# Retention into a mixture of experts on one core: the decay multiplication of both tiles of a pair put behind both tiles' outputs, one-hots and weight splits put behind the masks, and k of the first four tiles turned on TensorE

## The chip, the cores and the metric

The kernel runs on one core of a Trainium2 chip. The metric is device time in microseconds (us), from the start of the program on the core to its end; a smaller one is better. In the tables of the profile the engines are PE (TensorE, the matmuls), PEld (TensorE's weight loads), DVE (VectorE), ACT (ScalarE), POOL (GpSimd) and SP (the engine that issues the DMAs of this kernel).

## What is computed

The output of a retention layer (causal attention without softmax, with a decay gamma^(i-j) for each head) goes as tokens into a mixture of eight experts, one expert for each token.

```python
def _attn_ref(q, k, v):                      # batch 8, heads 8, seq 576, head_dim 64
    scores = scale * np.matmul(q, k.transpose(0, 1, 3, 2))
    gamma = 1.0 - 2.0 ** (-5.0 - np.arange(H))
    rel = pos[:, None] - pos[None, :]
    Dmat = np.where(rel >= 0, gamma[:, None, None] ** rel[None, :, :], 0.0)
    return np.matmul(scores * Dmat[None, :, :, :], v)

def _moe_ref(x, expert_emb, tau, w1, w2):    # x: 4608 tokens of 512
    logits = xn @ en.T / tau
    expert_idx = np.argmax(logits, axis=1)
    gate_w = probs[np.arange(N), expert_idx]
    for e in range(E):                       # 8 experts, w1 512x1024, w2 1024x512
        mask = expert_idx == e
        h = np.maximum(x[mask] @ w1[e], 0.0)
        out[mask] = gate_w[mask, None] * (h @ w2[e])
    return out
```

## The kernel before

The 4608 tokens are 36 tiles of 128 rows, nine tiles to two batches of 576 (tile 4 of the nine lies half in each batch). The retention takes the tiles in 18 **pairs**: pair s holds the tiles t = 2s and u = 2s + 1. All operands are float32. q and k come transposed (`qkt`, 512 KB for a tile), k and v also as rows (`kvt`, 512 KB for a tile: k in half 0, v in half 1). The steps for a tile, by the functions' names:

- `emit_A` (scores): TensorE multiplies k and q into two banks of PSUM, pa[0] and pa[1] for an even tile, pa[2] and pa[3] for an odd one; then VectorE multiplies each bank by the triangle `tri` (L614, the **masks**, four for a pair) into SBUF.
- `emit_U` (state): TensorE adds k-rows times v to the running state in the bank `pst`; ScalarE copies it to `T` (L690). v has been scaled by gamma^-i before, by GpSimd (`scale_v`, L597).
- `emit_QT` and `emit_O` (output): TensorE adds T times q, and the masked scores times v, in `po`. `po` is one tile of two banks, and each bank holds halves of both tiles of the pair.
- `emit_X` (L700): VectorE multiplies the output in `po` by the decay `gsb` into `xT` in SBUF. This is **the decay multiplication**.
- `emit_T`: TensorE turns `xT` back to rows (L134, into `prow` and pa[3]), ScalarE copies them (L716) and squares them (L719), and a DMA stores them in `xd` (L717).

In pair s the program writes: loads of the tiles t+5 and u+5, `scale_v` of t+2 and u+2, A of t+2 and u+2, QT of t and u, U of u, O of t, X of t, O of u, U of t+2, X of u, then T of the pair before. Loads, `scale_v` and A thus run ahead of the outputs. The order within an engine is the order of this text (`manual_schedule`); the waits between engines are set by the framework from the tiles that an instruction reads and writes.

Between these steps stand **jobs**, hung at a place (pair, slot) by `at` and run by `do`: slot 0 is ahead of the loads, slot 1 behind A, slot 2 behind the outputs, slot 3 at the end of the pair. They route the tokens, group by group of four or five tiles: logits (TensorE), turn and head (VectorE), rank, `route_onehot` (VectorE, L315, L323, L330: the **one-hots**) and `route_table` (TensorE). Four more are **weight splits**: ScalarE rounds a quarter of the first expert's w1 (L191), VectorE forms the rest (L192). Three prepare the experts' embeddings (square, a sum on TensorE, scale). In front of the loop stand tile 0 and A of tile 1; A of the tiles 2 and 3 is in pair 0.

Behind the retention come the experts: gather tokens, two layers of matmuls for each expert, scatter. The change doesn't touch them.

Of the kernel before, what the change touches and what calls it, by code (L numbers as in the profile page):

```python
# [47 lines left out]
LAST = 2  # L48
KT = 9
NLOAD = 7  # L50
PORD = (0, 2, 1, 3)


# [40 lines left out]
def retention_moe(ctx: ExitStack, tc: tile.TileContext, qk, kv, embT, tau, w1, w2, cst, out):  # L94
# [389 lines left out]
    with ExitStack() as att:  # L484
# [12 lines left out]
        def load_qk(t):  # L497
            qkt[t] = qkp.tile([P, NP, 2, P], F32, name="qkt")
            nc.sync.dma_start(out=qkt[t], in_=qk[t])

        def load_kv(t):
            kvt[t] = qkp.tile([P, 2, H, D], F32, name="kvt")
            nc.sync.dma_start(out=kvt[t], in_=kv[t])

        emb = ap.tile([P, NP, NE], F32, name="emb")
        taub = ap.tile([P, 1], F32, name="taub")
# [4 lines left out]
        nc.sync.dma_start(out=cs[:, _FIRST:], in_=cst[:, _FIRST:])  # L511
        load_kv(1)
        load_qk(2)
        nc.sync.dma_start(out=emb, in_=embT)
        nc.sync.dma_start(out=taub, in_=tau.rearrange("(o n) -> o n", o=1).broadcast_to([P, 1]))
        load_kv(2)
        for t in range(3, NLOAD):
            load_qk(t)
            load_kv(t)

# [16 lines left out]
        nc.vector.memset(E32, 0.0)  # L537
        nc.gpsimd.memset(vx[:D], 0.0)
        nc.vector.tensor_scalar(out=tri, in0=iota, scalar1=part, scalar2=None, op0=ALU.is_ge)

        def constants():
            nc.vector.tensor_scalar(out=ident, in0=iota, scalar1=part, scalar2=None, op0=ALU.is_equal)
            nc.vector.tensor_copy(trix, tri)
            nc.vector.memset(trix[:D, D:], 0.0)
            nc.vector.tensor_scalar(out=stri, in0=iota, scalar1=part, scalar2=None, op0=ALU.is_gt)
            nc.vector.tensor_scalar(
                out=wme, in0=iota[:, :NE], scalar1=-1.0, scalar2=float(NE), op0=ALU.mult, op1=ALU.add
            )
            nc.vector.tensor_scalar(out=entry[:, :, 0], in0=iota[:, :NT], scalar1=1.0, scalar2=None, op0=ALU.add)
            nc.vector.tensor_scalar(  # L550
                out=entry[:, :, 1], in0=iota[:, :NT], scalar1=0.0, scalar2=part, op0=ALU.mult, op1=ALU.add
            )
# [68 lines left out]
        def out_rows(p, h):  # L621

            o = h ^ (p & 1)
            return slice(o * D, (o + 1) * D)

        opened = set()

# [135 lines left out]
                f()  # L763

        at((0, 3), constants)
        at((0, 3), lambda: (embeddings_square(), embeddings_sum()))
        at((1, 3), embeddings_scale)
        for b in range(B - 1):
            t0, G = group_tiles(b)
            s0 = (t0 + G - 1) // 2 + 1  # L770
            if b < B - 2:
                at((s0, 2), lambda b=b: route_logits(b))
                at((s0, 3), lambda b=b: (route_turn(b), route_head(b)))
                at((s0 + 1, 3), lambda b=b: (route_rank(b), route_onehot(b)))
                at((s0 + 2, 3), lambda b=b: route_table(b))
            else:
                at((s0 - 1, 3), lambda b=b: route_logits(b))
                at((s0, 1), lambda b=b: (route_turn(b), route_head(b)))
                at((s0, 3), lambda b=b: (route_rank(b), route_onehot(b)))
                at((s0 + 1, 1), lambda b=b: route_table(b))  # L780
                at((s0 + 1, 1), lambda: slots_to_tokens(0, 3))
                for i in range(3):
                    at((s0 + 1, 1), lambda i=i: gather(0, i, group_tiles(B - 1)[0] * P))
                at((s0 + 1, 1), route_bump)
        for i, (load, split) in enumerate(wsplit_steps(0, wrp)):
            at((5 + 2 * i, 0), load)
            at((8 + 2 * i, 3), split)

        def loads(t):
            if t < NT:  # L790
# [1 line left out]
                load_kv(t)  # L792

        emit_A(0)
        scale_v(0, nc.vector)
        emit_U(0)
        decay(0)
        scale_v(1, nc.gpsimd)
        decay(1)
        emit_A(1)  # L800
        for s in range(NT // 2):
            t, u = 2 * s, 2 * s + 1
            do(s, 0)
            if s > 0:
                loads(t + NLOAD - 2)
                loads(u + NLOAD - 2)
                scale_v(t + 2, nc.gpsimd)
                scale_v(u + 2, nc.gpsimd)
                for k in (t + 2, u + 2):
                    if k < KT:  # L810
                        decay(k)
                if s < NT // 2 - 1:
                    emit_A(t + 2)
                    emit_A(u + 2)
            else:
                scale_v(2, nc.gpsimd)
                scale_v(3, nc.gpsimd)
                decay(2)
                decay(3)
            psm.banks = [prow]  # L820
            do(s, 1)
            psm.banks = [pa[2], pa[1], pa[0]]
            emit_QT(t)
            emit_QT(u)
            emit_U(u)
            emit_O(t)
            emit_X(t)
            emit_O(u)
            emit_U(t + 2)
            emit_X(u)  # L830
            if s == 0:
                emit_A(2)
                emit_A(3)
            do(s, 2)
            if s > 0:
                emit_T(t - 2)
                emit_T(u - 2)
            do(s, 3)
# [352 lines left out]
```

## Time and profile before

| | |
|---|---|
| time, median of 3 runs | 638.23 us (637.53 to 641.52) |
| the profiled execution: time | 638.23 us |
| the profiled execution: span of its instructions | 636.4 us |
| PE busy | 591.1 us (93%) |
| PEld busy | 527.6 us (83%) |
| DVE, ACT, POOL busy | 318.8, 223.0, 191.1 us |
| HBM read, written | 82.08 MB, 19.94 MB |

The span is that of the instructions in the trace; 1.8 us of the execution lie outside it. The retention takes about the first 195 us, the experts the rest. A busy matmul's end is modelled, so weight loads (PEld), which stand ahead of each matmul, tell more exactly where TensorE has nothing to do.

### The profile page before, as it was taken

The page shows a single profiled execution, that of the slowest core. Times are in us where ns is not written, and L with a number is a line of the kernel's source. Part 1 is how long each engine was busy: PE and PEld are TensorE (multiplying, and loading weights), DVE is VectorE, ACT ScalarE, POOL GpSimd, SP SyncE. Part 2 cuts the span into 40 slices and gives each one's busy share as a digit, 9 for nine tenths or more (in the row PEclk, how much of TensorE's full clock was granted, in tenths as well). Part 3 has the DMA queues.
Part 4 walks back from the last instruction along what each step waited for, and adds up shares of the span by engine and source line. Part 5 has one row for each costly group of instructions (what it writes and reads, how often), then busy time and mean ns, then how long its engine had stood idle before and what let it go on. Part 6 is the DMA issues. An engine that isn't in the chain of part 4 may idle for free.

```text
span 636.4 us, 12682 instructions
## 1 busy us (share of the span) xinstructions
PE 591.1 (93%) x5154; PEld 527.6 (83%) x5154; DVE 318.8 (50%) x626; ACT 223.0 (35%) x427; POOL 191.1 (30%) x184
## 2 busy tenths in 40 slices
PE   7798887787778999999999999999999999999995
PEld 6677776676656989998898899899889899989985
DVE  3456565756652757857147417626724633731200
ACT  1043423333524325624242425432623434241211
POOL 3743123112114175540450314234235032320002
PEclk8799997989987999999999999999999999999998
DMA  8768886687415296968429616737725651910001
GB/s 309 303 234 313 322 301 260 231 316 295 154 50 183 76 246 175 301 144 194 149 80 205 217 42 154 247 105 155 249 80 145 171 200 41 195 74 35 2 8 70
DMA packets 76324, 111.89 MB, mean 176 GB/s; under 512 B 44971, under 2 KB 45263, under 8 KB 76241
## 3 DMA queue, kind: packets, MB, share of 16 engines
q1 hardware_dynamic: 68560, 90.74, 45.4%
q0 software_dynamic: 7680, 19.95, 9.8%
q8 instruction: 63, 1.03, 0.6%
q14 instruction: 21, 0.16, 0.1%
HBM read 82.08 MB, written 19.94 MB: 160 GB/s over the span
## 4 chain that ended last, share of the span: by engine, by line
PE 66%; issue 15%; DVE 10%; DMA 3%; ACT 3%; POOL 3%; SPq 1%; POOLq 0%; DVEq 0%; ACTq 0%
PE pa L130 20%; PE o L926 20%; PE po L130 7%; PE prow L130 7%; PE pst L130 6%; PE pa L926 3%; DVE raw L614 3%; DVE xT L700 2%; DVE wslot L192 2%; PE prow L134 2%; PE pa L134 1%; DMA kvt<-kv 1%; POOL out L934 1%; DMA raw<-raw 1%; POOL gt L393 1%
## 5 line engine op out<-in xcount | busy, mean ns | idle before, releaser
L926 PE MATMUL o<-wslot,hs 128*128 128x512 f32 (+1 forms) x816 | 186.6, 384 | 0.5 <-ACT y L933 0.4
L926 PEld LDWEIGHTS o<-wslot,hs 128*128 128x128 f32 x816 | 148.6, 188 | 29.5 <-ACT y L933 0.8
L130 PE MATMUL pa<-xs,wslot 128*128 128x256 f32 (+4 forms) x912 | 132.9, 298 | 0.0
L130 PEld LDWEIGHTS pa<-xs,wslot 128*128 128x128 f32 x912 | 127.3, 190 | 0.9
L934 POOL DMA_INDIRECT out<-y,sid x40 | 43.5, 1088 | 223.3 <-ACT y L933 208.2
L192 DVE TENSOR_TENSOR wslot<-raw,wslot 128x1024 fp32r<-128x1024 f32 x64 | 78.6, 1233 | 32.2 <-ACT wslot L191 31.5
L866 DVE SCALAR_TENSOR_TENSOR hs<-pa,hs 128x384 fp32r<-128x384 f32 (+1 forms) x76 | 35.7, 477 | 104.5 <-ACT hs L865 104.5
L597 POOL TENSOR_TENSOR kvt<-kvt,cs 128x512 f32<-128x512 f32 x35 | 36.9, 1055 | 106.0 <-DMA kvt<-kv 83.0
L191 ACT CAST wslot<-raw 128x1024 fp32r<-128x1024 f32 x64 | 66.4, 1048 | 6.0 <-DMA raw<-w 5.4
L865 ACT ACTIVATE hs<-pa 128x256 fp32r<-128x256 f32 (+1 forms) x76 | 32.3, 433 | 98.6 <-PE pa L130 90.1
L382 POOL DMA_INDIRECT raw<-xd,gid x40 | 43.3, 1082 | 78.3 <-DVE wslot L192 29.6
L130 PE MATMUL po<-raw,kvt 128*64 128x128 f32 (+1 forms) x640 | 42.4, 281 | 22.9 <-DVE xT L700 21.3
L933 ACT ACTIVATE y<-o,gt 128x512 f32<-128x512 f32 (+1 forms) x34 | 22.6, 674 | 106.7 <-PE o L926 93.7
L130 PEld LDWEIGHTS po<-raw,kvt 128*64 128x64 f32 x640 | 34.4, 146 | 27.7 <-DVE xT L700 24.9
L130 PE MATMUL prow<-xs,wslot 128*128 128x320 f32 (+4 forms) x336 | 55.5, 314 | 0.2 <-issue 0.2
L130 PEld LDWEIGHTS prow<-xs,wslot 128*128 128x128 f32 x336 | 51.9, 188 | 1.4 <-issue 0.5
L690 ACT COPY T<-pst 128x256 f32<-128x256 f32 x32 | 11.9, 372 | 108.5 <-PE pst L130 108.5
L393 POOL DMA_INDIRECT gt<-gd,gid x40 | 45.3, 1133 | 12.2 <-issue 12.2
L130 PE MATMUL pa<-qkt 64*128 64x128 f32 x576 | 44.6, 294 | 3.8 <-ACT lt L739 1.1
L130 PEld LDWEIGHTS pa<-qkt 64*128 64x128 f32 x576 | 39.4, 199 | 8.2 <-DVE L_all L749 2.1
L614 DVE TENSOR_TENSOR raw<-pa,tri 128x512 f32<-128x512 f32 x64 | 40.0, 682 | 10.2 <-PE pa L130 10.2
L700 DVE TENSOR_TENSOR xT<-po,gsb 128x512 f32<-128x512 f32 x36 | 24.8, 690 | 39.2 <-PE po L130 37.9
(140 smaller groups left out, 605.3 us busy)
## 6 DMA issues: line engine op xcount, KB each, us to landing
raw<-w SPq DMA_DIRECT2D x64, 512.0 KB, 4.3
qkt<-qk SPq DMA_DIRECT2D x36, 512.0 KB, 5.9
kvt<-kv SPq DMA_DIRECT2D x36, 512.0 KB, 6.6
xd<-y SPq DMA_DIRECT2D x36, 256.0 KB, 2.2
raw<-xd,gid POOLq DMA_INDIRECT x40, 3.6
gt<-gd,gid POOLq DMA_INDIRECT x40, 4.3
out<-y,sid POOLq DMA_INDIRECT x40, 3.1
raw<-raw SPq DMA_TRANSPOSE x37, 3.7
```

The costliest lines, as they stand in the source:

```text
L130: pe[:] = [nc.tensor.matmul(*args, **kw)]
L191: nc.scalar.copy(hi, raw)
L192: nc.vector.tensor_tensor(out=sl[:, 1, c * 1024 : (c + 1) * 1024], in0=raw, in1=hi.bitcast(F32), op=ALU.subtract)
L382: return nc.gpsimd.indirect_dma_start(out=t[:, :DM], out_offset=None, in_=xd[:rows, :], in_offset=bass.IndirectOffsetOnAxis(ap=gid[:, a : ...
L393: nc.gpsimd.indirect_dma_start(out=g[:, i : i + 1], out_offset=None, in_=gd[:, :], in_offset=bass.IndirectOffsetOnAxis(ap=gid[:, a : a + 1 ...
L597: eng.tensor_tensor(out=v, in0=v, in1=gneg[:, t % KT].unsqueeze(2).broadcast_to([P, H, D]), op=ALU.mult)
L614: nc.vector.tensor_tensor(out=pm[:, h], in0=banks[h].rearrange("p (c n) -> p c n", c=NP), in1=m.unsqueeze(1).broadcast_to([P, NP, P]), op= ...
L700: nc.vector.tensor_tensor(out=xg4[b][:, g], in0=po[:, :, t % 2], in1=gsb[:, t % KT].rearrange("p (o r) n -> p o (r n)", o=2), op=ALU.mult,)
L865: a = nc.scalar.activation(hi, ps[:, :n], AF.Relu)
L866: v = nc.vector.scalar_tensor_tensor(out=hs[:, 1, f, o : o + n], in0=ps[:, :n], scalar=0.0, in1=hi.bitcast(F32), op0=ALU.max, op1=ALU.subt ...
L926: nc.tensor.matmul(ps[:, :step], hs[:, hsp, f, i * P : (i + 1) * P], w[:, ws, f, n : n + step], start=(f == 0 and k == 0), stop=(f == NF - ...
L934: sc = nc.gpsimd.indirect_dma_start(out=out[:, :], out_offset=bass.IndirectOffsetOnAxis(ap=sid[:, a : a + 1], axis=0), in_=y, in_offset=No ...
```

## The change

Three things are moved and one is done in another way.

- `emit_X` of both tiles stands behind O of both tiles and U of t+2. In pair 0, A of the tiles 2 and 3 stands ahead of U of tile 2.
- `route_onehot` goes from slot 3 of a pair (behind the outputs, ahead of the next pair's masks) to slot 1 of the next pair (behind its masks), the weight splits from slot 3 to slot 1 of the same pair. The three steps of the embeddings come later, each in a place of its own.
- For the first four tiles only v is loaded as rows (256 KB instead of 512 KB). Their k-rows are made from the transposed k: four transposes on TensorE into `prow` and one copy on ScalarE (`turn_k`), ahead of U. For this the identity `ident` is made earlier.
- The order of the first loads: `emb` and `taub` come later.

```diff
         def load_kv(t):
             kvt[t] = qkp.tile([P, 2, H, D], F32, name="kvt")
-            nc.sync.dma_start(out=kvt[t], in_=kv[t])
+            if t < TURNED:
+                nc.sync.dma_start(out=kvt[t][:, 1], in_=kv[t][:, 1])
+            else:
+                nc.sync.dma_start(out=kvt[t], in_=kv[t])
...
+        def turn_k(t):
+            if t < TURNED:
+                for p in range(NP):
+                    tr(prow[:, p * P : (p + 1) * P], qkt[t][:, p, 1, :], ident)
+                nc.scalar.copy(kvt[t][:, 0].rearrange("p h d -> p (h d)"), prow)
...
-        at((0, 3), lambda: (embeddings_square(), embeddings_sum()))
-        at((1, 3), embeddings_scale)
+        at((1, 1), embeddings_square)
+        at((1, 3), embeddings_sum)
+        at((2, 1), embeddings_scale)
...
-                at((s0 + 1, 3), lambda b=b: (route_rank(b), route_onehot(b)))
+                at((s0 + 1, 3), lambda b=b: route_rank(b))
+                at((s0 + 2, 1), lambda b=b: route_onehot(b))
                 at((s0 + 2, 3), lambda b=b: route_table(b))
...
-            at((8 + 2 * i, 3), split)
+            at((8 + 2 * i, 1), split)
...
         emit_A(0)
+        turn_k(0)
...
         emit_A(1)
+        turn_k(1)
...
             emit_O(t)
-            emit_X(t)
             emit_O(u)
-            emit_U(t + 2)
-            emit_X(u)
             if s == 0:
                 emit_A(2)
+                turn_k(2)
                 emit_A(3)
+                turn_k(3)
+            emit_U(t + 2)
+            emit_X(t)
+            emit_X(u)
             do(s, 2)
```

What this does to the order of the instructions is seen at three places. On TensorE in pair 5 the instructions before are these (`po<-qkt,T` is QT, `po<-raw,kvt` is O, `pst` is U; what an instruction waits for stands in brackets):

```order
L130 MATMUL po<-qkt,T 64x128 x16
L130 MATMUL pst<-kvt 64x64 [waits DMAHW7_49,Pool_49]
L130 MATMUL pst<-kvt 64x64 x7
L130 MATMUL po<-raw,kvt 64x128 x8
L130 MATMUL po<-raw,kvt 64x128 [waits DVE_49]
L130 MATMUL po<-raw,kvt 64x128 x7
L130 MATMUL pst<-kvt 64x64 [waits DMAHW1_49,Activation_49,Pool_49]
```

The same place in the changed kernel:

```order
L131 MATMUL po<-qkt,T 64x128 x16
L131 MATMUL pst<-kvt 64x64 [waits DMAHW7_49,Pool_49]
L131 MATMUL pst<-kvt 64x64 x7
L131 MATMUL po<-raw,kvt 64x128 x16
L131 MATMUL pst<-kvt 64x64 [waits DMAHW1_49,Activation_49,Pool_49]
L131 MATMUL pst<-kvt 64x64 x7
L131 MATMUL pa_72<-xT,E_203 32x512 [waits DVE_49]
```

O of both tiles is now one run of 16 matmuls, and the wait for VectorE in its middle is gone; the next wait for VectorE in this pair is that of the logits.

On VectorE, from the end of pair 8 on, before (`bt`, `ra` and `rp` are the one-hots, `wslot` is the weight split, `raw<-pa` are the masks of pair 9, `xT` its decay multiplications):

```order
L315 TENSOR_TENSOR bt<-ai,cs 128x512 [waits DVE_49]
L323 TENSOR_TENSOR ra<-ai,cs 128x160
L330 TENSOR_TENSOR rp<-ra,entry 128x320 [waits DVE_49]
L192 TENSOR_TENSOR wslot_84<-raw,wslot_84 128x1024 [waits DMAHW2_49,Activation_49]
L614 TENSOR_TENSOR raw<-pa_70,tri 128x512 [waits PE_49]
...
L614 TENSOR_TENSOR raw<-pa_73,tri 128x512 [waits PE_49]
L700 TENSOR_TENSOR xT<-po,gsb 128x512 [waits PE_49] x2
```

In the changed kernel, from the last mask of pair 8 on:

```order
L620 TENSOR_TENSOR raw<-pa_73,tri 128x512 [waits PE_49,Activation_49]
L193 TENSOR_TENSOR wslot_84<-raw,wslot_84 128x1024 [waits DMAHW2_49,Activation_49]
L712 TENSOR_TENSOR xT<-po,gsb 128x512 [waits PE_49]
L712 TENSOR_TENSOR xT<-po,gsb 128x512
...
L620 TENSOR_TENSOR raw<-pa_73,tri 128x512 [waits PE_49,Activation_49]
L316 TENSOR_TENSOR bt<-ai,cs 128x512 [waits DVE_49]
L324 TENSOR_TENSOR ra<-ai,cs 128x160
L331 TENSOR_TENSOR rp<-ra,entry 128x320 [waits DVE_49]
L712 TENSOR_TENSOR xT<-po,gsb 128x512 [waits PE_49]
L712 TENSOR_TENSOR xT<-po,gsb 128x512
```

The split now runs behind the masks of pair 8, the one-hots behind those of pair 9, and only the first of a pair's two decay multiplications waits for TensorE.

On TensorE between A of tile 3 and A of tile 4, before (`pa_71<-sq,onef` is the sum of the embeddings):

```order
L130 MATMUL pa_73<-qkt 128x128
L130 MATMUL pa_71<-sq,onef 128x8 [waits DVE_49]
L130 MATMUL pa_71<-sq,onef 128x8 x3
L130 MATMUL pa_70<-qkt 128x128 [waits DMAHW4_49]
L130 MATMUL pa_71<-qkt 128x128 [waits DVE_49]
```

And in the changed kernel (`prow<-ident,qkt` turns k of tile 3, `pst` is U of tile 2):

```order
L131 MATMUL pa_73<-qkt 128x128
L135 MATMUL prow<-ident,qkt 128x128 [waits Activation_49]
L135 MATMUL prow<-ident,qkt 128x128 x3
L131 MATMUL pst<-kvt 64x64 [waits Pool_49]
L131 MATMUL pst<-kvt 64x64 x7
L131 MATMUL pa_70<-qkt 128x128 [waits DMAHW4_49,DVE_49]
L131 MATMUL pa_71<-qkt 128x128 [waits DVE_49]
```

The sum with its wait has left this place (it stands at the end of pair 1), and turning and U have come in.

## Rows read from the trace of the kernel before

**Rows 1.** The page, 40 equal slices of the span: TensorE's granted clock in tenths.

```profile
PEclk8799997989987999999999999999999999999998
```

**Rows 2.** Who waited for whom, 0 to 190 us: total us, times, longest.

```profile
PEld po L130 <- DVE xT L700: 24.9, 16, 3.7
```

**Rows 3.** Timeline, pairs 3 and 4: start, us, engine, operation [idle before <- releaser].

```profile
45.57 1.10 PE L130 MATMUL po<-qkt,T 64*64 64x128 f32 x32
...
47.06 0.86 PEld L130 LDWEIGHTS po<-raw,kvt 128*64 128x64 f32 x16
...
48.29 0.69 DVE L700 TENSOR_TENSOR xT<-po,gsb 128x512 f32<-128x512 f32 x1 [0.90 <-PE po L130]
49.03 0.85 PEld L130 LDWEIGHTS po<-raw,kvt 128*64 128x64 f32 x16 [1.11 <-DVE xT L700]
...
50.25 0.69 DVE L700 TENSOR_TENSOR xT<-po,gsb 128x512 f32<-128x512 f32 x1 [1.27 <-PE po L130]
...
54.13 0.67 PE L130 MATMUL po<-qkt,T 64*64 64x128 f32 x16
```

**Rows 4.** Timeline: O of the second tile in pairs 7 and 17, start of pair 16.

```profile
93.76 0.88 PEld L130 LDWEIGHTS po<-raw,kvt 128*64 128x64 f32 x16 [1.06 <-issue]
...
172.25 0.48 PE L130 MATMUL pa<-qkt 64*128 64x128 f32 x2
...
191.25 1.60 PEld L130 LDWEIGHTS po<-raw,kvt 128*64 128x64 f32 x16 [1.22 <-issue]
```

**Rows 5.** Timeline: pair 9 from the weight split on, and one row of pair 11.

```profile
99.51 1.95 DVE L192 TENSOR_TENSOR wslot<-raw,wslot 128x1024 fp32r<-128x1024 f32 x1
...
101.38 2.47 DVE L614 TENSOR_TENSOR raw<-pa,tri 128x512 f32<-128x512 f32 x4
...
104.50 1.98 PE L130 MATMUL po<-raw,kvt 128*64 128x128 f32 x16 [3.42 <-DVE xT L700]
...
109.56 0.97 PE L134 MATMUL prow<-ident,xT 128*128 128x128 f32 x4
...
127.81 1.98 PE L130 MATMUL po<-raw,kvt 128*64 128x128 f32 x16 [2.73 <-DVE xT L700]
```

**Rows 6.** Timeline: the same two steps in pair 5.

```profile
65.86 1.09 PE L130 MATMUL po<-raw,kvt 128*64 128x128 f32 x16 [0.80 <-DVE xT L700]
...
68.56 0.66 PE L134 MATMUL prow<-ident,xT 128*128 128x128 f32 x4
```

**Rows 7.** Timeline: A of tiles 2 and 3, then pair 1 to its end.

```profile
16.02 2.06 PE L130 MATMUL pa<-qkt 64*128 64x128 f32 x32
...
21.21 1.54 PEld L130 LDWEIGHTS pa<-sq,onef 128*128 128x128 f32 x8 [3.33 <-DVE sq L558]
...
22.78 4.11 PE L130 MATMUL pa<-qkt 64*128 64x128 f32 x32
...
26.81 1.82 PE L130 MATMUL po<-qkt,T 64*64 64x128 f32 x32
...
33.50 1.38 PE L130 MATMUL pa<-qkt 64*128 64x128 f32 x18
```

**Rows 8.** Busy us by engine in two stretches, granted clock, DMA share, GB/s.

```profile
36.00:162.00 126.00, 106.07 (x1837) 89.69 (x1835) 76.11 (x173) 46.56 (x111) 30.35 (x30) 0.96 0.79 287
84.00:99.00 15.00, 13.62 (x218) 11.59 (x222) 8.73 (x26) 6.77 (x16) 3.13 (x3) 1.00 0.89 321
```

**Rows 9.** DMA issues, 0 to 190 us: count, KB each, median us to landing.

```profile
qkt<-qk SPq DMA_DIRECT2D x36, 512.0 KB, 5.9
kvt<-kv SPq DMA_DIRECT2D x36, 512.0 KB, 6.6
xd<-y SPq DMA_DIRECT2D x32, 256.0 KB, 2.2
raw<-w SPq DMA_DIRECT2D x4, 512.0 KB, 3.3
```

**Rows 10.** Waits of SP's own queue, 0 to 200 us.

```profile
SPq L186 <- DVE wslot L192: 6.1, 2, 3.3
```

More of the change, by code (lines that the diff above doesn't have):

```diff
@@ L50 @@
 NLOAD = 7
+TURNED = 4
 PORD = (0, 2, 1, 3)
@@ L513, in retention_moe @@
         load_qk(2)
+        load_kv(2)
         nc.sync.dma_start(out=emb, in_=embT)
+        load_qk(3)
+        load_kv(3)
         nc.sync.dma_start(out=taub, in_=tau.rearrange("(o n) -> o n", o=1).broadcast_to([P, 1]))
-        load_kv(2)
-        for t in range(3, NLOAD):
+        for t in range(4, NLOAD):
             load_qk(t)
@@ L539, in retention_moe @@
         nc.vector.tensor_scalar(out=tri, in0=iota, scalar1=part, scalar2=None, op0=ALU.is_ge)
+        nc.vector.tensor_scalar(out=ident, in0=iota, scalar1=part, scalar2=None, op0=ALU.is_equal)
         def constants():
-            nc.vector.tensor_scalar(out=ident, in0=iota, scalar1=part, scalar2=None, op0=ALU.is_equal)
             nc.vector.tensor_copy(trix, tri)
```

## The prediction

> **What bounds the kernel now.** I first read the granted clock in 40 slices of 15.9 us [rows 1]. It is full for the experts, from the fourteenth slice on, and dips only in the thirteen ahead: the retention is where TensorE runs dry. Then the list of waits up to 190 us [rows 2]: TensorE's weight loads for the output `po` stood idle 24.9 us behind the decay multiplication `xT`, in 16 waits. That is the longest wait of TensorE, and it is the one that the change is about.
>
> The timeline shows its form [rows 3]. In pair 3 the weight loads of O of the first tile run from 47.06 to 47.92. VectorE multiplies the first tile's output from 48.29 to 48.98, and only at 49.03 do the weight loads of the second tile's O begin: 1.11 us of nothing. The second tile writes other columns of the same two banks, so the program makes it wait. 16 of the 18 pairs have this wait by name; in the pairs 7 and 17 the same gap is there under "issue", 1.06 and 1.22 us [rows 4].
>
> The longest of these waits (3.7 us) is in pair 9. There VectorE still does a weight split (99.51, 1.95 us) before the pair's masks (101.38, 2.47 us), the first tile's multiplication stands behind both, and TensorE starts the second tile at 104.50, after 3.42 us. It starts at the lower clock level: O of one tile takes 1.98 us, against 1.09 in pair 5 [rows 5, 6].
>
> DMA is busy but not the bound: 0.79 of the engines' time between 36 and 162 us at 287 GB/s [rows 8].
>
> **The change, part by part.**
>
> *The wait in the outputs.* With both O ahead of both multiplications, the weight loads of the second tile follow those of the first. I take the weight loads' idle time, since a matmul's end is modelled: 24.9 + 1.06 + 1.22 = 27.2 us [rows 2, 4]. That includes the long waits, as nothing of VectorE stands ahead of O of the second tile any more but its masks, done a pair before. From below: the matmuls' own idle time is less, 0.80 in pair 5 [rows 6] where I count about 1.1, so 18 x 0.3 = 5.4 us may not come.
>
> What is late next is the multiplication itself. Now both run behind the second O. In pair 3 the second tile's O began at 49.03, its multiplication at 50.25; two in a row end at 50.25 + 2 x 0.69 = 51.63, 2.6 us after that O began. The next QT, which writes `po` again, began at 54.13, 5.1 us after it [rows 3]. So 2.5 us are left, and I count nothing. In a pair with a split the masks and the split take 2.47 + 1.95 = 4.4 us of VectorE [rows 5]; from QT to the end of two O's weight loads TensorE needs 47.06 - 45.57 + 2 x 0.86 = 3.2 us [rows 3]. The multiplications may start 1.2 us late, inside the 2.5.
>
> In the two pairs without a U of t+2 (3 and 12) the rank of a group stands close behind the multiplications on VectorE, and A of the next pair waits for it. One more multiplication ahead of it costs up to 0.69 each; I take 0.7 for both, ends 0 and 1.4.
>
> A rule speaks against this part. In row terms: today the multiplication of one tile does not overlap the O of the other at all (48.98, then 49.03) [rows 3]. The Trainium skill (Perfetto Trace Analysis, Matmuls) says that independent groups of matmuls should rotate through different PSUM banks, so that the evacuation of one overlaps the matmuls of the next; putting the evacuations behind both groups gives that up. By the trace there is no overlap to give up; what the rule would cost if it held is the third rival.
>
> *The clock.* In pair 9 from the second O to the turning it took 109.56 - 104.50 = 5.06 us, in pair 5 68.56 - 65.86 = 2.70; the turning itself 0.97 against 0.66. That is 2.7 us lost to the lower level behind the long wait. Pair 11 has the same in its O: 1.98 - 1.09 = 0.9 [rows 5, 6]. Both waits go, so I count 3.6 us. The lower end is 0, if the clock falls elsewhere.
>
> *The start.* Ahead of pair 1 TensorE waits 3.33 us for the embeddings' square, which stands on VectorE behind four masks and the constants, then sums them in 22.78 - 21.21 = 1.57 us. This moves to the end of pair 1, where the square is long done; the sum costs some 0.8 there, half of 1.57, as an estimate at the full clock. A of the tiles 4 and 5 then ran at the lower level, 4.11 us against 2.06 for the same work, and QT 1.82 against 1.10 [rows 3, 7]: 2.05 + 0.72. Against this stand four turnings of k at 0.66 each (the four transposes of [rows 6]), 2.6 us. Sum: 3.33 + 1.57 - 0.8 + 2.05 + 0.72 - 2.6 = 4.2 us. Without the clock it is 1.5; with turnings that cost only their spacing, and U of tile 2 no longer waiting for GpSimd, it may be 6.
>
> The copies of the turned k lie on ScalarE, which has little to do there; U of the first two tiles waits for them, but also for v to be scaled, so I count nothing (each may cost 0.6). Four loads of 256 KB less are 1.05 MB, at 321 GB/s [rows 8] 3.3 us by which all later loads of the start land earlier. No wait of TensorE in [rows 7] is for a load, so I count 0.
>
> *One-hots and splits behind the masks.* Their gain is in the long waits, counted above. SP waited 6.1 us for two splits before it could load the next weights [rows 10], with four loads of tiles queued behind; now the splits of the pairs 8 and 10 run before SP comes to the loads of 9 and 11. That evens the transfers and is not on the path. ScalarE's rounding moves with the split, ahead of the copy of `T`, in a time in which it waits for TensorE anyway.
>
> *The transfers.* Between the start of pair 2 (33.50) and of pair 16 (172.25) lie 138.75 us [rows 4, 7]. In them 27 tiles of 1 MB, 28 stores of 256 KB and 4 loads of weights of 512 KB move [rows 9]: 28.3 + 7.3 + 2.1 = 37.7 MB. The waits of these 14 pairs are 27.2 less four waits outside of about 1.1 each, 22.8; with the clock's 3.6, TensorE would need 112.4 us, hence 335 GB/s. The stretch of 36 to 162 us moved 287 at a share of 0.79, that is 363 at a full share; the fullest one, 84 to 99 us, 321 at 0.89 [rows 8]. At 363 the transfers need 104 us and hide; at 321 they need 117.5 and cost 5.1. I take 1.0, nearer to the full share, as DMA had idle time even in the fullest stretch.
>
> **Sum.** 27.2 + 3.6 + 4.2 - 0.7 - 1.0 = 33.3 us. The profiled execution took 638.23 us, which is also the median of the three runs; its span is 636.4. The new span is 603.1, the time 604.9 us, 5.2% less. The experts' part starts earlier by this and keeps its length, as no engine of it is fed differently.
>
> **The rivals.**
> 1. *The transfers become the bound.* For it: the share is high, loads are issued only one to two pairs ahead, and a pair gets shorter by 1.1 us with the same bytes. Against it: the gaps in the share. If they go no faster than the mean of 36 to 162 us, 287 GB/s, they need 131.4 us and give back 131.4 - 112.4 = 19, 18 more than I took: 622.9 us. Halfway, 614.
> 2. *The start gains nothing*, as the turnings, their copies and the wait for GpSimd fill the time: 604.9 + 4.2 = 609.1 us.
> 3. *The evacuations are exposed.* If something behind the two multiplications cannot wait 2.5 us, as the last logits or a turning, each pair pays one of 0.69: 18 x 0.69 = 12.4, 617.3 us. Against it: the matmuls next in order read what was multiplied a pair before. This is what the rule of the Trainium skill on banks above amounts to here.
> 4. *Slower.* Its place is A of the second tile ahead in each pair, whose load was issued a pair before. If shorter pairs let that load be late by as much as the wait of pair 9 (3.42 us), TensorE stands still and then runs at the lower level, 2.7 us lost on top: 6.1 us in each of 14 pairs is 85, against a gain of 33. It decides from the point at which 6 of 14 pairs (6 x 6.1 = 37) pay this: 604.9 + 37 = 642 us and more. Against it: transfers at their mean rate cost 19 us in all, 1.4 in a pair, and no such wait is in the trace.
> 5. *The change does not do what it says*: another wait for VectorE stands in the same place. The order of the instructions shows none ahead of the second O. It would leave the start's 4.2: 634 us.
>
> **How the numbers follow.** My forecast has 0.76, rival 1 0.12, rival 2 0.06, rival 3 0.03, rival 4 0.02, rival 5 0.01. The forecast's own ends are 600 (start 6, no cost of rank and transfers, pair 11 the same 2.7 as pair 9) and 611 (transfers 5.1 and some of the 5.4 of the matmuls' ends). With half of rival 1 the range is 600 to 616; beyond are the other half of rival 1, rivals 3 to 5 and the tails, under 0.2. About 1%, 6.4 us, is what a measurement of this kernel tells from no change. Faster by over 1%: 0.97, only rivals 4 and 5 are outside; within 1%: 0.01; slower: 0.02.
>
> **What the new profile would show.** Right: weight loads for `po` with no idle behind `xT`, O of both tiles as one group of 32, granted clock full between 100 and 140 us, pair 2 starting near 27 to 28 us, the first expert's matmuls some 33 us earlier, a DMA share near 0.9 in the pairs. Wrong: TensorE waits named after the loads of `qkt` or `kvt` (rival 1, or 4 if the clock falls with them), waits of `prow` or `pst` in the first 20 us (rival 2), QT or logits behind `xT` (rival 3). Most of all the prediction would be wrong by the transfers' rate, which no stretch before shows without idle time.

## The result, and the profile after

The changed kernel takes 602.56 us (median of four runs, 601.35 to 604.76), the kernel before 637.88 us (634.75 to 641.52): ratio 0.9448, 95% interval 0.9391 to 0.9506. Its profiled execution took 602.39 us with a span of 600.6, 35.8 less than before. The forecast was 604.9 us.

The page of the changed kernel, granted clock and DMA share in 40 slices of 15.0 us:

```profile
PEclk9999999999799999999999999999999999999999
DMA  8999999992437496963395167456518625610001
```

One dip is left, where retention passes into the experts; against [rows 1] those of the start and of the pairs 9 to 11 are gone, and DMA stands at nine tenths or more from the second slice to the ninth.

Timeline of pair 3 and the head of pair 4, the place of [rows 3] (line numbers have moved: L712 is the decay multiplication, L620 the masks, L193 the split):

```profile
37.83 1.92 PE L131 MATMUL po<-raw,kvt 128*64 128x128 f32 x32
...
40.29 1.29 DVE L712 TENSOR_TENSOR xT<-po,gsb 128x512 f32<-128x512 f32 x2 [1.99 <-PE po L131]
...
42.60 1.86 PEld L131 LDWEIGHTS pa<-qkt 64*128 64x128 f32 x30 [1.53 <-DVE t L295]
...
44.58 0.67 PE L131 MATMUL po<-qkt,T 64*64 64x128 f32 x16
```

O of both tiles is now one group of 32 without a gap, the two multiplications end at 41.58, and QT, which writes `po` again, begins 3.0 us later. The wait at 42.60 has grown: scores wait for the rank of a group, whose last steps on VectorE now stand behind both multiplications. Before, the same scores of pair 4 waited 0.70 us:

```profile
52.15 1.86 PEld L130 LDWEIGHTS pa<-qkt 64*128 64x128 f32 x30 [0.70 <-DVE t L294]
```

Of the list of waits of TensorE's weight loads, 25 to 170 us (in all, times, longest), these are the two largest that name VectorE inside the pairs 2 to 15; no line of the list names `xT`:

```profile
PEld pa L131 <- DVE t L295: 2.6, 3, 1.5
PEld pa L131 <- DVE L_all L761: 2.1, 5, 0.6
```

Pairs 8 and 9, where [rows 5] had the longest wait:

```profile
79.16 1.21 DVE L193 TENSOR_TENSOR wslot<-raw,wslot 128x1024 fp32r<-128x1024 f32 x1
...
83.30 2.48 DVE L620 TENSOR_TENSOR raw<-pa,tri 128x512 f32<-128x512 f32 x4 [0.55 <-PE pa L131]
...
85.21 1.92 PE L131 MATMUL po<-raw,kvt 128*64 128x128 f32 x32
```

The split now lies in pair 8, and O of pair 9 runs at the full clock beside the masks. The start, as in [rows 7]:

```profile
17.65 2.06 PE L131 MATMUL pa<-qkt 64*128 64x128 f32 x32
...
19.64 1.10 PE L131 MATMUL po<-qkt,T 64*64 64x128 f32 x32
...
24.73 0.96 PE L131 MATMUL pa<-sq,onef 128*128 128x8 f32 x8
...
25.61 2.38 PE L131 MATMUL pa<-qkt 64*128 64x128 f32 x32
```

The last row is the start of pair 2, 7.9 us earlier than in [rows 7]. DMA in the busiest stretch (columns as in [rows 8]):

```profile
29.00:135.00 106.00, 102.35 (x1911) 89.98 (x1908) 80.67 (x186) 49.16 (x115) 35.96 (x37) 1.00 0.95 347
```

The timelines cut the span into stages, for this kernel and for most of the experiments. "Pairs 2 to 15" runs from the scores at the head of pair 2 to those at the head of pair 16; "end" from there to the first matmul of an expert (`pst<-xs,wslot`):

```
kernel          start  pairs 2 to 15   end   first expert
before          33.50     138.75      31.21     203.46
before_again    34.43     135.58      31.21     201.22
x_only          32.92     116.08      27.28     176.28
jobs_only       32.52     129.23      30.84     192.59
start_only      27.81     135.09      28.40     191.30
unturned        29.35     112.06      27.34     168.75
emb_back        28.83     113.21      26.02     168.06
jobs_back       26.02     114.79      27.24     168.05
rank_first      26.04     111.92      27.30     165.26
changed         25.61     112.74      28.07     166.42
```

So of the 37.0 us by which the experts start earlier, 7.9 lie in the start, 26.0 in the pairs 2 to 15, 3.1 behind them. The experts' part is 1.2 us longer (434.2 against 433.0).

### The profile page after: what moved, and what is told of

The parts are those of the page before. It is cut to its first block, busy times and chain, and to the rows that moved or that the text cites. A ratio compares the mean times of both kernels' runs of the same rounds, so it can differ in the third digit from the quotient of the medians.

```text
span 600.6 us, 12718 instructions
## 1 busy us (share of the span) xinstructions
PE 579.1 (96%) x5170; PEld 520.1 (87%) x5170; DVE 318.7 (53%) x626; ACT 225.1 (37%) x431; POOL 191.2 (32%) x184
## 4 chain that ended last, share of the span: by engine, by line
PE 75%; issue 14%; DVE 5%; POOL 3%; ACT 2%; DMA 1%; POOLq 0%; DVEq 0%; ACTq 0%
PE pa L131 24%; PE o L944 21%; PE prow L131 8%; PE po L131 8%; PE pst L131 8%; PE pa L944 4%; PE pa L135 2%; PE prow L135 2%; POOL out L952 1%; POOL gt L394 1%; DVE wslot L193 1%; DVE xT L712 1%; DVE xs L406 1%; DVE raw L620 1%; DMA raw<-raw 1%
## 5 line engine op out<-in xcount | busy, mean ns | idle before, releaser
L193 DVE TENSOR_TENSOR wslot<-raw,wslot 128x1024 fp32r<-128x1024 f32 x64 | 77.8, 1221 | 32.7 <-ACT wslot L192 31.0
L884 DVE SCALAR_TENSOR_TENSOR hs<-pa,hs 128x384 fp32r<-128x384 f32 (+1 forms) x76 | 35.8, 478 | 103.2 <-ACT hs L883 99.7
L603 POOL TENSOR_TENSOR kvt<-kvt,cs 128x512 f32<-128x512 f32 x35 | 38.4, 1098 | 74.2 <-DMA kvt<-kv 68.1
L620 DVE TENSOR_TENSOR raw<-pa,tri 128x512 f32<-128x512 f32 x64 | 40.0, 682 | 14.4 <-PE pa L131 14.3
L131 PE MATMUL pa<-qkt 64*128 64x128 f32 x576 | 41.6, 282 | 4.8 <-DVE t L295 2.2
L131 PEld LDWEIGHTS pa<-qkt 64*128 64x128 f32 x576 | 36.6, 187 | 9.1 <-DVE t L295 2.6
L131 PE MATMUL pst<-xs,wslot 128*128 128x256 f32 (+1 forms) x288 | 42.3, 290 | 0.6 <-issue 0.3
L131 PEld LDWEIGHTS pst<-xs,wslot 128*128 128x128 f32 x288 | 38.7, 191 | 1.3 <-DVE xs L406 0.4
L702 ACT COPY T<-pst 128x256 f32<-128x256 f32 x32 | 11.9, 372 | 64.6 <-PE pst L131 64.5
L131 PE MATMUL po<-raw,kvt 128*64 128x128 f32 (+1 forms) x640 | 35.6, 266 | 0.0
```

What stands on the lines that cost most here:

```text
L131: pe[:] = [nc.tensor.matmul(*args, **kw)]
L193: nc.vector.tensor_tensor(out=sl[:, 1, c * 1024 : (c + 1) * 1024], in0=raw, in1=hi.bitcast(F32), op=ALU.subtract)
L603: eng.tensor_tensor(out=v, in0=v, in1=gneg[:, t % KT].unsqueeze(2).broadcast_to([P, H, D]), op=ALU.mult)
L620: nc.vector.tensor_tensor(out=pm[:, h], in0=banks[h].rearrange("p (c n) -> p c n", c=NP), in1=m.unsqueeze(1).broadcast_to([P, NP, P]), op= ...
L884: v = nc.vector.scalar_tensor_tensor(out=hs[:, 1, f, o : o + n], in0=ps[:, :n], scalar=0.0, in1=hi.bitcast(F32), op0=ALU.max, op1=ALU.subt ...
```

## The experiments

The kernels below were measured at different times, each beside the kernel before, whose median was 637.9 to 640.5 us; so their ratios are compared, and where the intervals overlap that of the changed kernel (0.939 to 0.951), the traces decide.

**The multiplications alone** (x_only), on the kernel before:

```
             emit_O(t)
-            emit_X(t)
             emit_O(u)
             emit_U(t + 2)
+            emit_X(t)
             emit_X(u)
```

> The kernel before with one edit: O of the second tile and U of t+2 stand ahead of both decay multiplications; one-hots, splits, loads and the start stay as before. Theory (the wait of O of the second tile behind the first multiplication was the cost, and it goes with this edit alone, the long waits of the pairs 9 and 11 and the clock with it): 27.2 + 3.6 - 0.7 - 1.0 = 29 us less, some 609 us, ratio 0.954. Rival (the long waits need the one-hots and splits moved too): only the common wait goes, 18 x 1.1 to 1.5 = 20 to 24 us and no clock, 614 to 618 us; then waits of QT or of the next scores behind VectorE or a load behind SP's wait for a split show in the pairs 8 to 15.

Measured: 610.5 us, ratio 0.954 (0.946 to 0.962). The theory holds. Pair 9 of its timeline:

```profile
91.89 1.22 DVE L192 TENSOR_TENSOR wslot<-raw,wslot 128x1024 fp32r<-128x1024 f32 x1
92.24 1.92 PE L130 MATMUL po<-raw,kvt 128*64 128x128 f32 x32
93.03 2.48 DVE L614 TENSOR_TENSOR raw<-pa,tri 128x512 f32<-128x512 f32 x4
...
95.42 1.27 DVE L700 TENSOR_TENSOR xT<-po,gsb 128x512 f32<-128x512 f32 x2
...
97.91 2.56 PE L130 MATMUL pa<-qkt 64*128 64x128 f32 x32
```

Split and masks stand ahead of the multiplications as before, but O no longer waits for any of them, and pair 9 (from 88.98) takes 8.9 us instead of 14.8. Of the rival's signs some are there, at a smaller size: in pair 13 scores wait for a load.

```profile
125.90 1.16 PE L130 MATMUL pa<-qkt 64*128 64x128 f32 x16 [1.30 <-DMA qkt<-qk]
```

**The jobs alone** (jobs_only), on the kernel before:

```
-                at((s0 + 1, 3), lambda b=b: (route_rank(b), route_onehot(b)))
+                at((s0 + 1, 3), lambda b=b: route_rank(b))
+                at((s0 + 2, 1), lambda b=b: route_onehot(b))
...
-            at((8 + 2 * i, 3), split)
+            at((8 + 2 * i, 1), split)
```

> The kernel before with one edit: one-hots and weight splits behind the pair's masks on VectorE. Theory (splits and masks both stand ahead of the first multiplication in either order, so the long wait stays): 637 to 639 us, no difference. Rival (the order of masks and split makes the long waits and the clock's fall): the waits beyond 1.1 us each go, 24.9 - 16 x 1.1 = 7.3, and the clock's 3.6, some 627 us, ratio 0.983.

Measured: 629.4 us, ratio 0.985 (0.976 to 0.994). The theory falls, the rival's size is right. Its pairs 8 and 9:

```profile
91.83 1.22 DVE L192 TENSOR_TENSOR wslot<-raw,wslot 128x1024 fp32r<-128x1024 f32 x1
...
93.75 1.09 PE L130 MATMUL po<-raw,kvt 128*64 128x128 f32 x16 [1.26 <-issue]
...
102.42 1.09 PE L130 MATMUL po<-raw,kvt 128*64 128x128 f32 x16 [1.38 <-DVE xT L700]
...
106.86 2.56 PE L130 MATMUL pa<-qkt 64*128 64x128 f32 x32
```

What counted was not the order against the masks but the pair. Before, pair 9 held the one-hots, the split and the masks ahead of its first multiplication. Here the split runs in pair 8, behind its masks (91.83) and beside O, and pair 9 keeps only the one-hots and the masks: its wait falls from 3.42 to 1.38 us, while that of pair 8 grows from 0.85 to 1.26.

**The start alone** (start_only): the changed kernel with the two edits above taken back.

> The kernel before with the start of the changed one: k of four tiles turned by TensorE and not loaded, the order of the first loads, the embeddings' three steps in other places, scores of the tiles 2 and 3 ahead of U of tile 2; multiplications and one-hots and splits as before. Theory: pair 2 starts 5.7 us earlier (the 7.9 us that the changed kernel showed less two waits of 1.1 behind the multiplications), 632 us, ratio 0.991; the later pairs keep their length. Rival (what came early at the start waits later, as loads or at the gathers): 636 to 638 us.

Measured: 629.3 us, ratio 0.986 (0.978 to 0.995). Pair 2 starts 5.7 us earlier, as expected. The pairs 2 to 15 are 3.7 us shorter too, 2.9 of it in pair 9, which is 11.89 us long (90.34 to 102.23) against 14.84, though its wait is there. That kernel's timeline, and then a window of it (columns as in [rows 8]):

```profile
97.79 1.09 PE L131 MATMUL po<-raw,kvt 128*64 128x128 f32 x16 [3.16 <-DVE xT L712]
```

```profile
100.00:115.00 15.00, 13.88 (x265) 12.15 (x259) 9.65 (x26) 7.63 (x18) 4.21 (x4) 1.00 0.75 286
```

The wait is nearly the same (3.16 against 3.42 us [rows 5]), and the clock is full. The kernel before had the same window at 0.77:

```profile
100.00:115.00 15.00, 11.55 (x153) 8.97 (x148) 8.53 (x19) 4.00 (x10) 3.95 (x4) 0.77 0.63 228
```

**The kernel before once more** (before_again), for a second trace (one execution):

> The kernel before, unchanged, for a second trace. Theory of the clock's term (the long wait of pair 9 makes the clock fall): the granted clock is again near 0.77 between 100 and 115 us and pair 9 takes some 14.8 us. Rival (where the clock falls changes from one execution to the next, as the kernel with only the start changed had the same wait and a full clock there): the wait of some 3.4 us is there and pair 9 takes some 12 us, at a full clock.

Its timeline, and the window:

```profile
104.86 1.98 PE L130 MATMUL po<-raw,kvt 128*64 128x128 f32 x16 [3.02 <-DVE xT L700]
```

```profile
100.00:115.00 15.00, 11.96 (x197) 9.83 (x188) 9.70 (x20) 4.02 (x11) 4.31 (x4) 0.89 0.66 244
```

Measured: 637.1 us. The trace lies between theory and rival: the wait is there, O behind it is at the lower level again, but the mean clock is 0.89 and pair 9 takes 13.05 us (97.70 to 110.75). Pair 9 with its wait thus took 14.8, 13.1 and 11.9 us in three traces, two of this kernel and that of start_only: the clock's share is 0 to 3 us, and not fixed by the wait.

**Without turning** (unturned), the changed kernel with one number changed:

```
-TURNED = 4
+TURNED = 0
```

> The changed kernel with k of the first four tiles loaded and not turned (no turnings, no copies of theirs; order of loads and all else as changed). Theory of the prediction (turnings cost TensorE their time, the start's gain comes from the embeddings and the clock): 0 to 2.6 us faster than the changed kernel, 600 to 602.5 us. Rival (the 1.05 MB that are not loaded bring tiles 2 and 3 earlier, and the turnings keep TensorE busy and its clock up): pair 2 starts later, and the time is 2 to 6 us more, 604 to 608 us.

Measured: 603.9 us, ratio 0.946 (0.937 to 0.954); the time alone doesn't tell it from the changed kernel. The trace does: pair 2 starts at 29.35, 3.7 us later. Its timeline ahead of that:

```profile
16.66 1.16 PE L131 MATMUL pa<-qkt 64*128 64x128 f32 x16 [0.66 <-DMA qkt<-qk]
...
20.00 1.16 PE L131 MATMUL pa<-qkt 64*128 64x128 f32 x16 [1.56 <-DMA qkt<-qk]
...
22.58 1.16 PE L131 MATMUL pa<-qkt 64*128 64x128 f32 x16 [1.42 <-DVE entry L556]
```

Scores of the tiles 3 and 4 wait for their loads, those of tile 5 for the constants. So the rival is right on pair 2: turning is worth its saved bytes. The clock is full there without turning too, so the rival's second ground, the clock, does not show. Turning gains 2.3 us at the first expert.

**The embeddings back** (emb_back), on the changed kernel:

```
-        at((1, 1), embeddings_square)
-        at((1, 3), embeddings_sum)
-        at((2, 1), embeddings_scale)
+        at((0, 3), lambda: (embeddings_square(), embeddings_sum()))
+        at((1, 3), embeddings_scale)
```

> The changed kernel with one part undone: the embeddings' square and sum back at the end of pair 0, their scaling at the end of pair 1. Theory by the trace of the changed kernel (the square would come on VectorE some 2.7 us after TensorE is free for the next scores, the sum takes 1.0 and no longer stands in pair 1): pair 2 starts 2.7 us later, some 605 us. Theory of the prediction (the square's wait of 3.33, the longer sum, and the clock's 2.8 behind it): 6.9 us, some 609 us, with a granted clock below full between 20 and 36 us.

Measured: 605.3 us, ratio 0.947 (0.942 to 0.952). Pair 2 starts 3.2 us later. The list of waits, and then a window, first of this kernel and then of the kernel before:

```profile
PEld pa L131 <- DVE sq L564: 2.4, 1, 2.4
```

```profile
20.00:36.00 16.00, 15.20 (x296) 13.39 (x296) 9.96 (x22) 4.00 (x10) 12.10 (x16) 1.00 0.68 265
```

```profile
20.00:36.00 16.00, 13.76 (x176) 12.67 (x176) 7.22 (x20) 3.25 (x8) 12.15 (x16) 0.79 0.55 217
```

The wait is back, but the clock stays full: the theory by the trace holds for pair 2, and the 2.8 us of the clock did not hang on this wait alone. At the first expert 1.6 us are left of it.

**The jobs back** (jobs_back), the changed kernel with the edit of jobs_only taken back:

> The changed kernel with one part undone: one-hots and weight splits back at the ends of their pairs. Theory (with the multiplications behind both O the place of these jobs matters only where VectorE's work in a pair is longer than the slack; the kernel with the multiplications alone needed 116.1 us for the pairs 2 to 15, the changed one 112.7): 3.3 us more, 605 to 606.5 us, and SP waits for splits again. Rival (that difference came from the start): 601 to 603.5 us. Second rival (these places matter as much as without the moved multiplications, where they gave 9.6 us): 610 us and more.

Measured: 604.7 us, ratio 0.946 (0.941 to 0.951), pairs 2 to 15 longer by 2.05 us. By the trace this is the theory, at two thirds of its size; the time alone doesn't tell it from the changed kernel. The waits of SP's queue (0 to 170 us; in all, times, longest), and the timeline:

```profile
SPq L187 <- DVE wslot L193: 5.7, 2, 3.0
```

```profile
116.67 1.16 PE L131 MATMUL pa<-qkt 64*128 64x128 f32 x16 [0.55 <-DMA qkt<-qk]
...
122.53 0.65 PE L135 MATMUL pa<-ident,xT 128*128 128x128 f32 x4 [0.69 <-DVE raw L620]
```

SP waits for two splits as in [rows 10]; in pair 13 scores wait 0.55 us for a load, and masks behind a split hold a turning by 0.7.

**The rank early** (rank_early), on the changed kernel:

```
-                at((s0 + 1, 3), lambda b=b: route_rank(b))
+                at((s0 + 1, 1), lambda b=b: route_rank(b))
```

> The changed kernel with one edit: the rank of a group (its matmuls and VectorE's small steps behind them) stands behind the masks of its pair and writes the bank prow, no longer at the pair's end in a bank that the next scores write. Theory (the scores of the pairs 4, 7, 9, 11, 13 and 16 wait for VectorE's rank step behind the two multiplications): the 2.6 us of these waits go, some 600 us. Rival (in the pairs 8, 10 and 12 masks, rank and split together make the multiplications late, and QT waits behind xT): no gain, 602 to 605 us, with waits of po for xT.

Measured: 602.7 us, ratio 0.945 (0.942 to 0.949). The waits for the rank are gone, the time is not. It was not the multiplications that came late. Its timeline:

```profile
37.07 0.18 PE L131 MATMUL prow<-oh,stri 128*128 128x32 bf16 x1 [0.38 <-DVE oh L229]
...
43.19 1.16 PE L131 MATMUL pa<-qkt 64*128 64x128 f32 x14 [0.15 <-ACT y L728]
```

TensorE now waits for the group's head just ahead, and the next scores come so early that they wait for ScalarE's copy out of their bank. The first expert starts 0.8 us later than in the changed kernel; small waits took the place of three larger ones.

**The rank first** (rank_first), on the changed kernel:

```
+            rank = s in (3, 8, 12)
+            if not rank:
+                emit_X(t)
+                emit_X(u)
             do(s, 2)
...
             do(s, 3)
+            if rank:
+                emit_X(t)
+                emit_X(u)
```

> The changed kernel with one edit: in the pairs 3, 8 and 12, which have a rank and no U of t+2, both multiplications stand behind the rank's small steps on VectorE. Theory (the scores of the next pair wait 2.6 us for the rank's product, which stands behind 1.3 us of multiplications; these have room until the next QT): the waits fall to some 0.3 us each, 1.5 to 2 us less, 600.5 to 601 us. Rival (QT now waits for the multiplications): no gain, 602 to 604 us, with waits of po for xT.

Measured: 601.05 us, ratio 0.941 (0.936 to 0.946). The waits, as above:

```profile
PEld pa L131 <- DVE t L295: 0.8, 2, 0.4
```

1.8 us of waits go, one of 0.6 us of `po` for `xT` comes in, and the experts start 1.2 us earlier. It has the lowest time of all, though its interval does not part it from the changed kernel.

**Each multiplication twice** (x_doubled), on the changed kernel:

```
-            nc.vector.tensor_tensor(
-                out=xg4[b][:, g],
+            for _ in range(2):
+                nc.vector.tensor_tensor(
+                    out=xg4[b][:, g],
...
```

> The changed kernel with each decay multiplication done twice (same result): VectorE has 1.3 us more per pair ahead of the next QT, 23 us in all. Theory of the prediction (2.5 us are left behind the multiplications, so their length is hidden): only what waits for rank and logits pays, 1.3 us in some 6 pairs, up to 8 us, 602 to 610 us. Rival (the evacuations are the path now): 18 x 1.3 = 23 us, some 626 us, with waits of QT or the logits behind xT in every pair.

Measured: 615.8 us, ratio 0.966 (0.962 to 0.970), between the two. Pair 12 of the timeline, and the list of waits:

```profile
124.26 2.74 DVE L713 TENSOR_TENSOR xT<-po,gsb 128x512 f32<-128x512 f32 x4 [0.70 <-PE po L131]
...
127.75 1.16 PE L131 MATMUL pa<-qkt 64*128 64x128 f32 x16 [1.32 <-DVE t L295]
...
128.84 0.67 PE L131 MATMUL po<-qkt,T 64*64 64x128 f32 x16
```

```profile
PEld pa L131 <- DVE t L295: 9.4, 5, 2.5
```

Even doubled, the multiplications (124.26 to 127.00) end 1.8 us ahead of the next QT, though 1.3 of that is the wait for the rank at 127.75. The cost, 13.3 us, is more than the theory's 8. What pays is what stands behind them on VectorE at the pair's end: waits for the rank grow from 2.6 to 9.4 us. The table of slots and the sum of the embeddings pay as well; of the loads for `po` one waits for `xT`, 0.7 us. Some 2.5 us more, by estimate, are the clock's: behind the longest wait for the rank the weight loads of 32 scores took 3.31 us against 1.86 in the same pair of the changed kernel, and those of 30 in pair 2, behind the embeddings, 2.93.

```profile
90.80 3.31 PEld L131 LDWEIGHTS pa<-qkt 64*128 64x128 f32 x32 [2.45 <-DVE t L295]
```

**More loads** (load_256, load_512), on the changed kernel, the second with two of these loads:

```
                 loads(u + NLOAD - 2)
+                if s < 14:
+                    nc.sync.dma_start(out=extra[s % 2], in_=kv[t][:, 0])
```

> The changed kernel with one more load of 256 KB in each of the pairs 1 to 13, into a tile that nothing reads: 3.4 MB. Theory (share 0.95 at 347 GB/s between 29 and 135 us, 365 at a full share: room for 1.9 MB): the other 1.5 MB cost 4.1 us, 606.5 us, with waits of TensorE or GpSimd for qkt and kvt. Rival (there is more room, as loads are issued early and the queue drains after pair 13): no cost, 601 to 604 us.

> The changed kernel with two more loads of 256 KB in each of the pairs 1 to 13: 6.8 MB, 4.9 MB beyond the room. Theory: 4.9 MB at 365 GB/s, 13.4 us, some 616 us. Rival (more room): less than 7 us, under 609 us. A steeper one: late loads let TensorE's clock fall, 620 us and more.

Measured: 601.9 us, ratio 0.944 (0.940 to 0.947), and 605.0 us, ratio 0.948 (0.945 to 0.952). The window of the first, then of the second:

```profile
29.00:135.00 106.00, 102.51 (x1913) 89.82 (x1903) 83.64 (x187) 49.14 (x115) 35.95 (x38) 1.00 1.00 378
```

```profile
29.00:135.00 106.00, 100.27 (x1835) 87.84 (x1828) 75.88 (x176) 47.04 (x110) 35.51 (x36) 0.98 1.02 393
```

3.4 MB more cost nothing, 6.8 MB cost 2.4 us by the medians, whose intervals overlap (5.6 in the span of its profiled execution). The rivals with more room hold; 365 GB/s was no ceiling. The share is no ceiling at 1 either, since it reads 1.02 in the second.

## Why the prediction was right, point by point

By the stages of the table, the sum had 6.4 us in the start (4.2 and two waits), 24.7 in the pairs 2 to 15 and 2.2 behind them; measured were 7.9, 26.0 and 3.1, less 1.2 in the experts. The pairs carry the result, and there the mechanism is shown. That the total came within 2.5 us is in part luck: terms missed by 1 to 2 us in both directions, as the points below show, and against the second trace of before the stages are 8.8, 22.8 and 3.1, less 0.1.

**The wait in the outputs (27.2).** Right in place and mechanism. The multiplications' edit alone took 28.5 us off the time; the sum for that edit was 29.1. The 5.4 us that might not have come (4.2 in these 14 pairs) mostly did. Against the second trace of before, whose clock fell less, the pairs 2 to 15 are 22.8 us shorter. With the 1.1 that waits for the rank grew, and without the 2.05 that the new places of the jobs give (jobs_back), 21.9 are left, against 22.3 of waits in that trace (25 to 170 us; the list holds one of pair 1 and lacks the one under "issue" in pair 8, both of 1.1) and 1.2 of the clock; so some 1.6 did not come:

```profile
PEld po L130 <- DVE xT L700: 22.3, 14, 3.3
```

The gap of 93.76 in [rows 4], which the prediction puts in pair 7, lies in pair 8 (88.38 to 96.78); the sum is not touched by it.

**The clock (3.6).** The mechanism is there, the size was taken from one execution. Three traces with the same wait in pair 9 lost about 3, 1.2 and 0 us to it. The changed kernel has a full clock through all pairs, so this gain comes, but its size is that of the execution it is compared with: the two traces of before differ by 3.2 us in the pairs 2 to 15.

**The start (4.2, and 2.2 of waits behind the multiplications).** Here a step failed. It gained 7.9, not 6.4. I had counted four turnings as 2.6 us of cost and the 1.05 MB not loaded as 0, because no wait of [rows 7] is for a load. Once other waits are gone and scores are moved ahead, loads are next: without turning, pair 2 starts 3.7 us later. The embeddings' places are worth 3.2 at a full clock, where I had 3.33 + 1.57 - 0.8 = 4.1 without the clock. These two and the 2.2 make 9.1, more than the 7.9 found even without the clock: the parts overlap, but where was not tested. The clock's 2.8 came too (0.79 before between 20 and 36 us, in both traces, and full in the changed kernel), but neither part taken back brings the lower level back, so it belongs to no single one of them.

**One-hots and splits.** "Their gain is in the long waits, counted above" is half of it. Alone they give 9.6 us, as they take the split out of the longest pair: the waits for `xT` fall from 22.8 to 17.3 us between 25 and 170 us, and the clock stays full in the pairs 2 to 15; the three parts alone give 28.5 + 9.6 + 9.6 = 47.7 us where all together give 35.3, in part because the multiplications and the jobs remove the same long waits (5.5 us of them by the list), in part because each alone is credited with the clock too (mean 1.00, 1.00 and 0.99 in the pairs 2 to 15 of the three traces, against 0.96 in the first trace of before). But with the multiplications moved, the jobs are still worth 2 us (SP's loads and masks that come late), which the sum did not hold.

**Behind the multiplications (0) and the rank (0.7).** The 2.5 us of slack are there: in the changed kernel no weight load waits for `xT`, and with the work doubled one of `po` does, for 0.7 us (where the rank delays QT, part of the slack is that wait). Waits for the rank grew by 1.1, from 1.5 to 2.6: by 0.8 behind pair 3 and 0.3 behind pair 8; the prediction had named the pairs 3 and 12. The kernel with the rank first gets 1.8 of all of them back. The third rival named the wrong followers, QT and logits; those that pay are small steps on VectorE whose bank the next scores write.

**The transfers (1.0).** They cost nothing. The full-share rate of 363 GB/s, worked out from [rows 8], was too low: with more bytes to move, the same stretch moved 378 and 393. This could have been read beforehand. The prediction takes 84 to 99 us, 321 GB/s, as the fullest stretch and says that no stretch before shows the transfers without idle time; but the start of that same trace, where only loads run, does:

```profile
8.00:23.00 15.00, 10.83 (x153) 9.55 (x154) 6.67 (x17) 1.12 (x3) 7.75 (x11) 0.84 1.02 401
```

At 401 GB/s the 37.7 MB need 94 us, 18 less than the 112.4 of the pairs. The first rival is out, and with it the fourth.

**The rest.** The end of retention gained 3.1 us, where the two waits of the pairs 16 and 17, 1.04 and 1.22, were counted. By the trace it is mostly the clock, which the prediction had not looked at there. The stretch "end" before and after:

```profile
172.25:203.46 31.21, 23.20 (x273) 18.13 (x269) 13.47 (x42) 12.11 (x29) 5.43 (x4) 0.78 0.28 98
```

```profile
138.35:166.42 28.07, 20.41 (x273) 16.16 (x269) 13.58 (x44) 12.11 (x29) 5.46 (x5) 0.88 0.35 119
```

The same 273 matmuls keep TensorE busy for 2.8 us less at a mean clock of 0.88 instead of 0.78; its idle time falls by only 0.3. The second trace of before has 0.78 there as well. The experts took 1.2 us back; that is no more than two traces of the kernel before differ by (433.0 and 434.1), so nothing has to be explained.

**The rule on banks.** The Trainium skill (Perfetto Trace Analysis, Matmuls) would have independent groups rotate through banks, so that an evacuation overlaps the next group. Here both tiles share their banks, and before no multiplication ran beside the other tile's O [rows 3], so the grouping gives up nothing; the traces show next to no cost of it (no wait for `xT`, and one of 0.7 us with the work doubled). One bank per tile was not tried.

## What to carry to other kernels

Where an evacuation between two groups of matmuls makes the second wait for the first because both write one bank, put both groups first, and then look at what stands behind the evacuations on their engine. Try each part alone and each part taken back: parts that remove the same wait add up to more than the whole, and a part that looks like cost (turning instead of loading) can pay once the wait ahead of it is gone. "No wait is for a load" holds only for the order in which it was read. And before a rate of transfers is taken from a busy stretch, look for a stretch of the same trace in which they do not pause.

## What the runs showed of the hardware

**VectorE's steps wait for GpSimd.** Some small ones last up to five times as long as usual. The changed kernel's timeline:

```profile
75.68 1.05 POOL L603 TENSOR_TENSOR kvt<-kvt,cs 128x512 f32<-128x512 f32 x1 [5.64 <-DMA kvt<-kv]
75.84 0.93 DVE L229 TENSOR_TENSOR oh<-wm,wme 128x32 bf16<-128x32 f32 x1
...
99.54 2.48 DVE L620 TENSOR_TENSOR raw<-pa,tri 128x512 f32<-128x512 f32 x4 [0.54 <-PE pa L131]
99.81 1.04 POOL L603 TENSOR_TENSOR kvt<-kvt,cs 128x512 f32<-128x512 f32 x1 [3.21 <-DMA kvt<-kv]
```

The small comparison of 0.19 us (in pair 3) takes 0.93 here and ends when GpSimd's multiplication does; the masks, which read a bank, take their usual 2.48 beside the same GpSimd work. Between 24 and 160 us eight VectorE steps last over a third longer than the median of their kind, 4.5 us more in all, and all eight lie beside work of GpSimd. The Trainium skill (SBUF — State Buffer, SBUF: two separate sides) tells of a port pair that the two share under an exclusive lock, for VectorE steps with two inputs in SBUF among others; the rows agree. The split of [rows 5] (99.51 to 101.46) lies beside GpSimd's work as well:

```profile
99.21 1.17 POOL L597 TENSOR_TENSOR kvt<-kvt,cs 128x512 f32<-128x512 f32 x1 [1.52 <-DMA kvt<-kv]
```

It took 1.95 us instead of the 1.21 of the changed kernel's pair 8: by this estimate, 0.7 of the long wait was GpSimd's.

**One core's transfers reach 393 GB/s** over 106 us (load_512), and 401 over 15 us at the start of the kernel before; 321 in [rows 8] was a stretch with pauses.
